# Early weight conversion: ScalarE's pass over the high words in place, VectorE's shift on every second word

## The chip, the cores and the metric

The kernel runs on one core of a Trainium2 chip. The metric is device time in microseconds (us), from the start of the program to its end. Times are compared as medians of several runs.

## The reference

Attention with pooled keys and values, then two feed-forward stages. Weights come as 64-bit floats; the matrix products are carried in two fp32r halves.

```python
def _attn_ref(q, k, v):            # B=8, H=8, S=576, D=64
    k_p = k.reshape(B, H, Sp, pool, D).mean(axis=3)      # pool = 8
    v_p = v.reshape(B, H, Sp, pool, D).mean(axis=3)
    scores = scale * np.matmul(q, k_p.transpose(0, 1, 3, 2))
    ...
    return np.matmul(attn, v_p)
...
def _moe_ref(x, w1, w2, w3, w_out):                      # x: 4608 x 512, d_ff 1024
    return (((x @ w1) * (x @ w2)) @ w3) @ w_out
...
def _moe2_ref(x, w_in, w_out):                           # d_ff 2048
    h = x @ w_in
    return (h * (1.0 / (1.0 + np.exp(-1.702 * h)))) @ w_out
```

## The kernel before, in words

Tokens are worked in nine blocks of 512. The kernel folds `w3 @ w_out` into one matrix first, then runs the blocks through `w1`, `w2` and that matrix (line L583 and on), while the attention of later heads runs beside it in "ticks", and then runs the second feed-forward stage.

**Conversion of the weights.** A weight tile is 128 x 512 numbers of 64 bits, loaded by SyncE (L151) into a slot `t` of shape 128 x 512 x 2 words: the low word and the high word of each number lie side by side. `Conv.step` turns it into fp32 in four operations. ScalarE reads the high words, every second word of the slot, and scales them (L166); ScalarE scales the low words in place (L168); VectorE shifts the result of L166 left by three bits (L169) into a tile `cv`; GpSimd adds the low words (L172). Then the slot is given back. There are four buffers of `cv`. Two steps later the tile is split into a rounded half and a rest (`split`: ScalarE L104, and VectorE or GpSimd L105). For `w3` TensorE transposes it first (L508). In the first stage 40 tiles are converted like this, `w_out`, `w3`, `w1` and `w2`. From the eighth block on `self.ps` holds two PSUM banks, and the result of L166 goes there: 32 more tiles, for the second feed-forward stage.

**Attention.** The work of one pair of heads, in steps that the ticks call: VectorE transposes k and q (L255, L256) and sums keys (L258); TensorE computes scores (L278); VectorE takes the maximum and subtracts (L283, L285); ScalarE takes the exponential (L294); VectorE sums and normalizes (L300 to L303) and transposes (L314, 20 instructions a pair); TensorE multiplies with the values (L380 to L383); ScalarE and VectorE write the result (L390, L391) into a slot that is one quarter of a block of x.

**Blocks.** For each of eight slices f of `w1` and `w2` TensorE does 12 matmuls (L114 to L116) into the bank `wk_70` and 12 into `wk_71`; ScalarE copies the first (L638), VectorE multiplies (L641). The next slice's matmuls into `wk_71` wait for L641.

**Order.** A scheduler builds the program once, from its own model of the timeline: it fixes the order of instructions on each engine, and each engine then works strictly in that order. An instruction that waits holds up everything behind it on its engine. So an edit in one place can move instructions that it doesn't touch.

Of the kernel before, what the change touches and what calls it, by code (L numbers as in the profile page):

```python
# [7 lines left out]
F32 = mybir.dt.float32  # L8
# [14 lines left out]
def pooled_attention_moe_moe2(  # L23
# [71 lines left out]
    def give(*ts):  # L95
        for t in ts:
            if id(t) in held:
                free.append(held.pop(id(t))[1:])
# [28 lines left out]
    class Conv:  # L127
# [27 lines left out]
        def step(self):  # L155

            new = None
            if self.staged:
                t, turn, done = self.staged.pop(0)
                lo_w, hi_w = t[:, :, 0], t[:, :, 1]  # L160
                w = cv_p[0].tile([P, T], F32, name="cv", tag="cv", bufs=4)
                wu = w.bitcast(U32)

                e = self.ps[self.n % len(self.ps)] if self.ps else w
                self.n += 1
                nc.scalar.activation(  # L166
                    e, hi_w.bitcast(F32), AF.Prelu, scale=2.0 ** -112, alpha=-2.0 ** 32)
                nc.scalar.activation(lo_w.bitcast(I32), lo_w, AF.Copy, scale=2.0 ** -29)  # L168
                nc.vector.tensor_scalar(  # L169
                    out=wu, in0=e.bitcast(U32), scalar1=3, scalar2=None,  # L170
                    op0=ALU.logical_shift_left)
                nc.gpsimd.tensor_tensor(  # L172
                    out=w.bitcast(I32), in0=w.bitcast(I32), in1=lo_w.bitcast(I32), op=ALU.add)
                give(t)
                new = [w, turn, done]
            mid, old = self.line
            if mid and mid[1]:
                mid[0] = mid[1](mid[0])
            key = old[2](old[0]) if old else None
            self.line = [new, mid]  # L180
            self.load()
            return key
# [489 lines left out]
    with tc.tile_pool(name="pb", bufs=1, reuse_waits="tile") as pb, \  # L672
# [206 lines left out]
        for k, f in enumerate(FO):  # L879
            bk = bank()  # L880
            w = ready.pop(("h", 0, f))
# [29 lines left out]
        for pr in range(1, NPAIR + 1):  # L911
# [12 lines left out]
            for fp in range(NFP):  # L924
# [4 lines left out]
                for name, i in ORDER:  # L929
# [6 lines left out]
                    if name in PART:  # L936
                        s, h = PART[name]
                        w = ready[s, pr, 2 * fp + i][:, h]
                    else:
                        w = ready[name, pr, fp][:, i]  # L940
# [156 lines left out]
```

## Time and profile before

| | us |
|---|---|
| median of 3 runs (1495.22 to 1498.04) | 1496.11 |
| profiled execution | 1496.16 |
| its span | 1494.0 |
| TensorE busy | 1441.0 |
| VectorE busy | 962.9 |
| ScalarE busy | 693.8 |
| GpSimd busy | 662.1 |

The span runs from the first to the last instruction of the profiled execution; 2.16 us of its time lie around the span. Busy times are shares of that span, and engines overlap.

### The profile page before, as it was taken

The page shows a single profiled execution, that of the slowest core. Times are in us where ns is not written, and L with a number is a line of the kernel's source. Part 1 is how long each engine was busy: PE and PEld are TensorE (multiplying, and loading weights), DVE is VectorE, ACT ScalarE, POOL GpSimd, SP SyncE. Part 2 cuts the span into 40 slices and gives each one's busy share as a digit, 9 for nine tenths or more (in the row PEclk, how much of TensorE's full clock was granted, in tenths as well). Part 3 has the DMA queues.
Part 4 walks back from the last instruction along what each step waited for, and adds up shares of the span by engine and source line. Part 5 has one row for each costly group of instructions (what it writes and reads, how often), then busy time and mean ns, then how long its engine had stood idle before and what let it go on. Part 6 is the DMA issues. An engine that isn't in the chain of part 4 may idle for free.

```text
span 1494.0 us, 19448 instructions
## 1 busy us (share of the span) xinstructions
PE 1441.0 (96%) x6536; PEld 1189.5 (80%) x6536; DVE 962.9 (64%) x1664; ACT 693.8 (46%) x1212; POOL 662.1 (44%) x653
## 2 busy tenths in 40 slices
PE   4988999999999999999999998999999999999998
PEld 3766888888888888888888876778877888788886
DVE  7888998878787877555627255583339433853354
ACT  6974444434343433365635344442455244534442
POOL 7787856555555555366833122500532043302530
PEclk9989999999999999999999999999999999999999
DMA  9991342323232311199879887767676866786665
GB/s 276 242 226 34 65 89 52 77 49 77 48 77 48 76 33 37 61 321 350 307 248 385 285 271 269 272 184 230 198 231 214 230 195 213 230 235 187 200 208 138
DMA packets 292323, 267.64 MB, mean 179 GB/s; under 512 B 199552, under 2 KB 224128, under 8 KB 292224
## 3 DMA queue, kind: packets, MB, share of 16 engines
q1 hardware_dynamic: 291648, 265.35, 59.0%
q10 hardware_dynamic: 576, 1.05, 0.2%
q8 instruction: 52, 0.85, 0.2%
q14 instruction: 47, 0.39, 0.1%
HBM read 209.72 MB, written 56.62 MB: 178 GB/s over the span
## 4 chain that ended last, share of the span: by engine, by line
PE 83%; DVE 6%; DMA 5%; ACT 2%; issue 2%; POOL 2%; SPq 0%; DVEq 0%; POOLq 0%; ACTq 0%
PE bk L709 38%; PE wk L114 8%; PE wk L116 8%; PE wk L115 8%; PE acc L114 5%; PE acc L116 4%; PE acc L115 4%; PE wk L278 2%; DMA xM<-x2d 2%; PE bk L115 1%; PE bk L116 1%; PE bk L114 1%; POOL cv L172 1%; DVE p L314 1%; DMA st<-wud 1%
## 5 line engine op out<-in xcount | busy, mean ns | idle before, releaser
L709 PE MATMUL bk<-mv,st 128*128 128x512 f32 x1104 | 263.6, 394 | 9.6 <-DVE mv L105 4.6
L709 PE MATMUL bk<-xM,st 128*128 128x512 f32 x1140 | 268.4, 390 | 1.9 <-ACT u L962 1.9
L709 PEld LDWEIGHTS bk<-mv,st 128*128 128x128 f32 x1104 | 209.2, 190 | 56.3 <-DVE mv L105 5.9
L709 PEld LDWEIGHTS bk<-xM,st 128*128 128x128 f32 x1140 | 214.4, 188 | 46.9 <-ACT u L962 2.3
L114 PE MATMUL wk<-s,s 128*128 128x512 f32 x576 | 228.1, 398 | 6.5 <-DVE a L641 3.8
L987 POOL TENSOR_TENSOR s<-g,s 128x1024 f32<-128x1024 f32 x16 | 38.8, 2423 | 426.0 <-ACT g L858 426.0
L115 PE MATMUL wk<-s,s 128*128 128x512 f32 x576 | 225.5, 392 | 0.1
L116 PE MATMUL wk<-s,s 128*128 128x512 f32 x576 | 225.3, 392 | 0.1
L314 DVE STREAM_TRANSPOSE p<-s_t 32x160 f32<-32x160 f32 (+1 forms) x560 | 178.5, 319 | 10.5
L105 POOL TENSOR_TENSOR s<-a,s 128x512 fp32r<-128x512 f32 x56 | 73.4, 1310 | 155.0 <-ACT s L104 121.2
L116 PE MATMUL acc<-s,s 128*128 128x512 f32 x352 | 139.4, 396 | 1.8 <-DVE s L105 1.8
L105 DVE TENSOR_TENSOR mv<-g,mv 128x1024 fp32r<-128x1024 f32 x80 | 112.9, 1411 | 43.8 <-ACT mv L104 42.6
L115 PE MATMUL acc<-s,s 128*128 128x512 f32 x352 | 139.5, 396 | 1.2 <-POOL s L105 1.1
L114 PE MATMUL acc<-s,s 128*128 128x512 f32 x352 | 131.9, 400 | 7.6 <-DVE s L105 4.5
L114 PEld LDWEIGHTS wk<-s,s 128*128 128x128 f32 x576 | 108.9, 189 | 30.8 <-DVE a L641 5.0
L116 PEld LDWEIGHTS wk<-s,s 128*128 128x128 f32 x576 | 108.7, 189 | 23.3 <-DVE s L105 0.5
L115 PEld LDWEIGHTS wk<-s,s 128*128 128x128 f32 x576 | 108.6, 189 | 22.2 <-DVE s L391 0.5
L172 POOL TENSOR_TENSOR cv<-cv,s 128x512 int32<-128x512 int32 x72 | 100.8, 1409 | 34.1 <-DVE cv L169 22.4
L104 ACT CAST mv<-g 128x1024 fp32r<-128x1024 f32 x80 | 84.1, 1053 | 64.9 <-PE bk L709 62.3
L114 PEld LDWEIGHTS acc<-s,s 128*128 128x128 f32 x352 | 66.7, 190 | 22.2 <-ACT s L104 5.0
L116 PEld LDWEIGHTS acc<-s,s 128*128 128x128 f32 x352 | 66.8, 190 | 15.6 <-DVE s L105 3.0
L115 PEld LDWEIGHTS acc<-s,s 128*128 128x128 f32 x352 | 66.8, 190 | 14.5 <-POOL s L105 2.3
(188 smaller groups left out, 2469.6 us busy)
## 6 DMA issues: line engine op xcount, KB each, us to landing
st<-wud SPq DMA_DIRECT2D x92, 512.0 KB, 4.2
st<-wind SPq DMA_DIRECT2D x66, 512.0 KB, 4.7
st<-wind SPq DMA_DIRECT2D x84, 256.0 KB, 4.0
s<-in_moe_w_dram SPq DMA_DIRECT2D x32, 512.0 KB, 6.2
wind<-s SPq DMA_DIRECT2D x32, 512.0 KB, 5.2
s<-in_moe_w_out_dram SPq DMA_DIRECT2D x24, 512.0 KB, 6.8
s<-wud SPq DMA_DIRECT2D x20, 512.0 KB, 4.5
kr<-in_k_dram SPq DMA_DIRECT2D x128, 72.0 KB, 2.5
```

What stands on the lines that cost most here:

```text
L104: nc.scalar.copy(dst[:, 0], src)
L105: lo_eng.tensor_tensor(out=dst[:, 1], in0=src, in1=f32(dst[:, 0]), op=ALU.subtract)
L114: nc.tensor.matmul(o, a[:, 0, a_sl], b[:, 0, b_sl], start=first, stop=False)
L115: nc.tensor.matmul(o, a[:, 0, a_sl], b[:, 1, b_sl], start=False, stop=False)
L116: nc.tensor.matmul(o, a[:, 1, a_sl], b[:, 0, b_sl], start=False, stop=last)
L172: nc.gpsimd.tensor_tensor(out=w.bitcast(I32), in0=w.bitcast(I32), in1=lo_w.bitcast(I32), op=ALU.add)
L278: nc.tensor.matmul(sc[half][:, i * KW:(i + 1) * KW], qT[:, sl(tt)], mov, start=True, stop=True)
L314: nc.vector.transpose(out=dst[:, :nt, 32 * c:32 * c + 32], in_=s_t[32 * c:32 * c + 32, :nt, 32 * r:32 * r + 32])
L709: nc.tensor.matmul(o, w[:, x, m], b[:, y], start=first and n == 0, stop=last and n == 2, skip_group_check=True)
L987: nc.gpsimd.tensor_tensor(out=o, in0=p, in1=m, op=ALU.subtract)
```

## The change

The result of L166 is written over the high words that it reads, in the slot, in place of going to the `cv` tile. VectorE's shift L169 then reads every second word of the slot and writes the `cv` tile, which is first used there. Where `self.ps` is set, nothing changes.

```diff
                 w = cv_p[0].tile([P, T], F32, name="cv", tag="cv", bufs=4)
                 wu = w.bitcast(U32)
 
-                e = self.ps[self.n % len(self.ps)] if self.ps else w
+                e = (self.ps[self.n % len(self.ps)] if self.ps else hi_w).bitcast(F32)
                 self.n += 1
                 nc.scalar.activation(
                     e, hi_w.bitcast(F32), AF.Prelu, scale=2.0 ** -112, alpha=-2.0 ** 32)
```

The scheduler builds another order from it. The first place is on TensorE, around the first block's first slice. `s_456`, `s_576`, `s_703` and `s_815` are the four quarters of that block of x; `ph`, `pt` and `vm`, `vt` belong to the attention that yields `s_815`; `s_1148` and `s_1173` are the first slice's weights.

```order
@@ -274,14 +274,6 @@
 L116 MATMUL wk_70<-s_703,s_1148 128x512
 L278 MATMUL wk_73<-kbd,qT 128x144 x2
-L380 MATMUL acc_68<-ph,vm 128x288
-L381 MATMUL acc_68<-ph,vm 128x288
-L380 MATMUL acc_69<-ph,vm 128x288
-L381 MATMUL acc_69<-ph,vm 128x288
 L114 MATMUL wk_71<-s_456,s_1173 128x512
 L115 MATMUL wk_71<-s_456,s_1173 128x512
-L382 MATMUL acc_68<-ph,vm 128x288
-L382 MATMUL acc_69<-ph,vm 128x288
-L383 MATMUL acc_68<-pt,vt 128x288
-L383 MATMUL acc_69<-pt,vt 128x288
 L278 MATMUL wk_72<-kbd,qT 128x144 x3
```

The eight matmuls of that attention stood ahead of `L278 wk_72`, which waits for a transposed q. They now come seven matmuls of 512 columns behind it:

```order
 L116 MATMUL wk_71<-s_703,s_1173 128x512
+L380 MATMUL acc_68<-ph,vm 128x288
+L381 MATMUL acc_68<-ph,vm 128x288
+L380 MATMUL acc_69<-ph,vm 128x288
+L381 MATMUL acc_69<-ph,vm 128x288
+L278 MATMUL wk_73<-kbd,qT 128x144 x2
+L382 MATMUL acc_68<-ph,vm 128x288
+L382 MATMUL acc_69<-ph,vm 128x288
+L383 MATMUL acc_68<-pt,vt 128x288
+L383 MATMUL acc_69<-pt,vt 128x288
 L114 MATMUL wk_70<-s_815,s_1148 128x512
```

So they are the last thing on TensorE before the first matmul that needs their result.

The second place is VectorE's queue at the same point of the program. Before, the two L391 that write `s_815` stand ahead of the maxima of the next scores, and the product L641 of the first slice comes nine rows behind them:

```order
130 L169 TENSOR_SCALAR cv<-cv 128x512
131 L105 TENSOR_TENSOR s_1444<-cv,s_1444 128x512
132 L300 TENSOR_REDUCE nm<-s_t 128x10
133 L283 TENSOR_REDUCE nm<-wk_73 128x4
134 L256 STREAM_TRANSPOSE qT<-qr 128x576
135 L391 TENSOR_TENSOR s_824<-acc_69,s_824 128x64
136 L258 TENSOR_REDUCE ks<-kT 128x72
137 L169 TENSOR_SCALAR cv<-cv 128x512
138 L641 TENSOR_TENSOR a<-wk_71,a 128x512
139 L301 TENSOR_SCALAR nm<-nm 128x10
```

Of the change:

```order
139 L283 TENSOR_REDUCE nm<-wk_73 128x4
140 L256 STREAM_TRANSPOSE qT<-qr 128x576
141 L258 TENSOR_REDUCE ks<-kT 128x72
142 L301 TENSOR_SCALAR nm<-nm 128x10
143 L105 TENSOR_TENSOR s_1581<-cv,s_1581 128x512
144 L255 STREAM_TRANSPOSE kT<-kr 128x576
145 L302 RECIPROCAL nm<-nm 128x10
146 L169 TENSOR_SCALAR cv<-s_1176 128x512
147 L391 TENSOR_TENSOR s_815<-acc_68,s_815 128x288
148 L391 TENSOR_TENSOR s_815<-acc_69,s_815 128x224
149 L303 TENSOR_TENSOR s_t<-s_t,nm 128x5x144
150 L391 TENSOR_TENSOR s_824<-acc_69,s_824 128x64
```

The L391 of `s_815` have moved from ahead of that L283 to eight instructions behind it. The third place follows on directly on VectorE: the first L641 now stands behind the 20 transposes of a pair of heads, of which these are the last.

```order
158 L314 STREAM_TRANSPOSE p_984<-s_t 32x4x32 x2
159 L314 STREAM_TRANSPOSE p_985<-s_t 32x5x32 x2
160 L314 STREAM_TRANSPOSE p_985<-s_t 32x4x32 x2
161 L641 TENSOR_TENSOR a<-wk_71,a 128x512
162 L169 TENSOR_SCALAR cv<-s_1241 128x512
163 L169 TENSOR_SCALAR cv<-s_1251 128x512
```

Before, both the first and the second L641 stood ahead of these transposes.

## Rows read from the trace of the kernel before

**Rows 1.** The page: span, and busy time of each engine.

```profile
span 1494.0 us, 19448 instructions
...
PE 1441.0 (96%) x6536; PEld 1189.5 (80%) x6536; DVE 962.9 (64%) x1664; ACT 693.8 (46%) x1212; POOL 662.1 (44%) x653
```

**Rows 2.** Busy time by stretch, then granted TensorE clock, DMA share, GB/s.

```profile
80.00:100.00 20.00, 17.69 (x78) 14.10 (x79) 17.53 (x24) 15.54 (x34) 18.29 (x22) 0.91 0.99 218
100.00:120.00 20.00, 15.47 (x59) 11.73 (x59) 17.79 (x29) 13.27 (x30) 16.05 (x21) 0.83 0.85 178
...
200.00:300.00 100.00, 100.00 (x481) 84.26 (x482) 86.88 (x214) 42.13 (x96) 58.28 (x81) 1.00 0.30 62
...
800.00:1494.00 694.00, 673.23 (x2937) 553.10 (x2935) 361.06 (x393) 298.35 (x392) 185.62 (x74) 0.99 0.72 227
```

**Rows 3.** Waits of TensorE to 180 us: total us, times, longest.

```profile
PE wk L508 <- POOL cv L172: 11.9, 3, 9.3
...
PE wk L114 <- DVE a L641: 3.8, 2, 1.9
```

**Rows 4.** The conversion's lines, each by itself: ns min/median/max.

```profile
L166 ACT ACTIVATE cv<-s x40: 642/668/693, 4.9 to 138.0; 128x512 f32<-128x512 f32 x40
L168 ACT ACTIVATE s<-s x72: 647/666/697, 5.5 to 728.4; 128x512 int32<-128x512 uint32 x72
L169 DVE TENSOR_SCALAR cv<-cv x40: 359/537/4302, 5.6 to 147.4; 128x512 uint32<-128x512 uint32 x40
L169 DVE TENSOR_SCALAR cv<-wk x32: 675/681/692, 632.6 to 745.7; 128x512 uint32<-128x512 uint32 x32
```

**Rows 5.** Groups of VectorE, 0 to 160 us: busy us, mean ns.

```profile
L169 DVE TENSOR_SCALAR cv<-cv 128x512 uint32<-128x512 uint32 x40 | 36.8, 929 | 10.1 <-ACT cv L166 10.1
```

**Rows 6.** GpSimd in order of time: start, us.

```profile
123.49 1.28 POOL L105 TENSOR_TENSOR s<-a,s 128x512 fp32r<-128x512 f32 x1
```

**Rows 7.** VectorE in order of time.

```profile
105.88 0.76 DVE L256 STREAM_TRANSPOSE qT<-qr 128x576 f32<-128x576 f32 x1
...
109.93 0.74 DVE L391 TENSOR_TENSOR s<-acc,s 128x288 fp32r<-128x288 f32 x2
...
113.70 0.44 DVE L283 TENSOR_REDUCE nm<-wk 128x4 f32<-128x288 f32 x1
...
117.70 1.26 DVE L105 TENSOR_TENSOR s<-cv,s 128x512 fp32r<-128x512 f32 x1
118.88 0.20 DVE L302 RECIPROCAL nm<-nm 128x10 f32<-128x10 f32 x1
120.76 4.30 DVE L169 TENSOR_SCALAR cv<-cv 128x512 uint32<-128x512 uint32 x1 [1.68 <-ACT cv L166]
124.98 1.16 DVE L303 TENSOR_TENSOR s_t<-s_t,nm 128x720 f32<-128x720 f32 x1
...
126.52 0.68 DVE L641 TENSOR_TENSOR a<-wk,a 128x512 f32<-128x512 f32 x1
127.12 6.64 DVE L314 STREAM_TRANSPOSE p<-s_t 32x160 f32<-32x160 f32 x20
```

**Rows 8.** The chain that ended last, followed from 96 to 130 us.

```profile
101.91 3.08 DMA qr<-in_q_dram
```

**Rows 9.** TensorE in order of time; in brackets the wait before.

```profile
106.79 1.78 PE L278 MATMUL wk<-kbd,qT 128*128 128x144 f32 x6 [2.07 <-DVE qT L256]
...
111.85 1.05 PE L114 MATMUL wk<-s,s 128*128 128x512 f32 x2
...
113.37 0.49 PE L115 MATMUL wk<-s,s 128*128 128x512 f32 x1
...
118.85 0.39 PE L114 MATMUL wk<-s,s 128*128 128x512 f32 x1
...
127.26 0.50 PE L114 MATMUL wk<-s,s 128*128 128x512 f32 x1 [1.90 <-DVE a L641]
...
147.53 0.50 PE L114 MATMUL wk<-s,s 128*128 128x512 f32 x1 [1.92 <-DVE a L641]
```

## The prediction

> **What bounds the kernel now.** The page comes first: TensorE is busy for 1441.0 of the 1494.0 us [rows 1], so what matters is where its other 53 us lie. The table by stretch answers that [rows 2]: from 200 to 300 us TensorE works for 100.00 of 100 us, and from 800 to the end for 673.23 of 694. The second figure leaves 21 us idle, in the second feed-forward stage, where the edit changes nothing (`self.ps` is set there). So the time that this change can win or lose lies in the first 200 us, and a lateness that TensorE takes out of them it keeps to the end, unless an idle place in the same stretch takes it back. From 80 to 100 us the DMA engines are busy for 0.99 of the time and from 100 to 120 us for 0.85: until there the loads set the pace. The waits of TensorE up to 180 us come next [rows 3]: 11.9 us before the transposes L508 of `w3`, and 3.8 us, in two waits, before the L114 that want `wk_71` back from L641. TensorE in order of time shows these two at 127.26 (1.90) and 147.53 (1.92), and one of 2.07 before the scores at 106.79 [rows 9]. That last one is for the transposed q of L256 (105.88), whose data lands at 101.91 + 3.08 = 104.99 [rows 7, 8]. An engine that is early before 105 us meets this DMA and gains nothing, and one that is late by up to 2.07 us loses nothing. Hence I follow the order behind 105 us and leave the reordering before it at nothing.
>
> **The change, part by part.** *ScalarE's pass.* L166 now writes every second word in place. L168 has that very shape (it reads and writes every second word) and takes 666 ns in the median, L166 now takes 668 [rows 4]: nothing.
>
> *VectorE's shift.* No row of the trace has VectorE reading every second word, so I bound it. The form in use, from `cv` to `cv`, takes 359 ns at least, 537 in the median, 4302 at most [rows 4], and 929 in the mean of the 40, together 36.8 us within the first 160 us [rows 5]. The spread is a wait inside the instruction. The one of 4.30 us begins at 120.76 and ends at 125.06, just behind a GpSimd subtraction that runs from 123.49 to 124.77 [rows 6, 7]. The form that reads PSUM lies within 675 to 692 ns in all 32 cases [rows 4]: slower by itself, never held. So the lower bound for the 40 new reads is the PSUM form's price without any wait, 40 x (929 - 681) = 9.9 us of VectorE less; the upper one is the slower read with today's waits kept, 40 x (681 - 359) = 12.9 us more. I take the price of today, 537 alone and 929 with the waits, because source and destination are still both in SBUF, as in the row with the wide spread, and only the step differs.
>
> The Trainium skill ("Vector Engine (DVE) Microarchitecture Reference", section 5.1, Performance modes) says that an operation with one source runs at two elements a cycle, over both ports, when source and destination lie in SBUF; the step is not among its conditions. "SBUF — State Buffer", section Who interferes with whom, says that such an operation and a GpSimd operation exclude each other. Here the trace agrees, by the 4.30 us beside the GpSimd row; that a step of two words keeps the mode, no row shows. By these pages the 40 reads cost what they do now, which speaks against a gain of VectorE's.
>
> *The wait for a `cv` buffer* moves from L166 on ScalarE to L169 on VectorE. Behind L169 stand maxima, transposes and L641. With four buffers and tiles freed two steps later I put it at nothing: in the timeline, the waits in front of L169 are for ScalarE (1.68 us at 120.76), not for a buffer [rows 7].
>
> *The order.* This is the part with a price. On TensorE the attention matmuls that yield `s_815` move behind `L278 wk_72`, which waits for the q at 104.99. On VectorE the two L391 that write `s_815` move from ahead of `L283 wk_73` (they ran at 109.93, that L283 at 113.70 [rows 7]) to eight instructions behind it. The first L641 moves behind the 20 transposes. Step by step:
> 1. q lands at 104.99; L256 starts at 105.0 (now 105.88). The L278 come 0.91 behind its start, as now (106.79 - 105.88 [rows 7, 9]): 105.9.
> 2. From there to the L114 of `s_815` TensorE needs 5.06 us (106.79 to 111.85 [rows 9]): 111.0. In their place now stand the first four attention matmuls, 288 columns each. Two L114 of 512 columns take 1.05 us [rows 9]; four of 288 are 1152 columns against 1024, and at a shorter pass I take 1.1: an estimate. Then `L278 wk_73`; today its maximum L283 starts at 113.70, 1.85 behind the L114 at 111.85, or 0.80 behind the 1.05 of the two. So L283 starts at 111.0 + 1.1 + 0.8 = 112.9.
> 3. VectorE then works through L283 0.44, L256 0.76, L258 0.76 (taken as L256, same number of columns), L301 0.20 (taken as L302), L105 1.26, L255 0.76 (as L256), L302 0.20, L169 0.54, and the L391 pair 0.74 [rows 4, 7]: 5.66. Neighbours overlap by about 0.08 (126.52 + 0.68 against 127.12 [rows 7]), nine times 0.7 in all. `s_815` is ready at 112.9 + 5.0 = 117.9. Now the pair ends at 110.67, and TensorE reads `s_815` from 111.85 on and goes on with it at 113.37 [rows 9]. I expect about 4 us of waiting there.
> 4. Behind it L303 1.16, an L391 of 64 columns 0.2 (as L302), and the 20 transposes, 6.64 [rows 7], less the overlaps: L641 starts at 125.6. TensorE follows 0.74 behind it (126.52 to 127.26 [rows 7, 9]): 126.35. That is the first matmul that needs `wk_71` free again, now at 118.85 without a wait [rows 9]. It is 7.5 us late.
> 5. What comes back: the transposes are now done earlier, so the next L641 no longer stand behind them, and the waits at 127.26 and 147.53 go: 1.90 + 1.92 = 3.8 us [rows 9]. Other idle time I see none to take from before 200 us.
>
> Sum: 7.5 - 3.8 = 3.7 us. The profiled execution takes 1494.0 + 2.16 = 1496.16 us, 0.05 above the median of the runs, so 1499.9; I say 1500.0. Without waits inside L105 and L169 it would be 0.8 less (1.26 to 0.68, the length of the L641 of the same size, and 537 to 359 ns [rows 4, 7]); if only one of the two waits goes, 1.9 more; if a shift in the queue ahead of `s_815` is held as long as the 4.30 us one, 3.8 more (4.30 - 0.54). The case's own range is 1499 to 1504.
>
> **The rivals.** A difference under 0.2%, or 3.0 us, can't be told from no change.
> - *No change.* The reordering pulls loads forward, and the q of step 1 lands earlier. For it: ScalarE no longer waits for `cv`. Against it: with 0.99 and 0.85 of the DMA engines busy, only 0.2 and 3.0 us of the 40 us from 80 to 120 can be won [rows 2]. All of it won gives 1500.0 - 3.2 = 1496.8. It decides from 0.9 us on, where the 3.8 falls under 3.0.
> - *Faster.* A read of every second word doesn't run in the form that waits for GpSimd, but as the one from PSUM: 681 ns, never held. All 9.9 us of VectorE on the path give 1500.0 - 9.9 = 1490.1. For it: VectorE is what the chain of steps 3 and 4 runs on, and the 4.30 us at 120.76 lie right before the L641 that TensorE awaits [rows 7]. Against it: both operands stay in SBUF. It comes out faster from 6.9 us on the path (3.9 + 3.0). The sign: L169 of at least 640 ns in the median with none over 700.
> - *Slower by more.* L169 is held often where `s_815` waits behind it, or the slow read keeps its waits as well (12.9 us in all): from 1504.5 up to 1500.0 + 12.9 = 1512.9. For it: the 4.30 us at 120.76 [rows 7]. Against it: the median of 537 ns, most tiles are hardly held [rows 4].
>
> The skill's rule on the two-port form, by which a strided read is still held by GpSimd, has its place in the forecast, and its failure is the second rival.
>
> **How the numbers follow.** Forecast, slower at about 1500.0: 0.50; slower by more: 0.05; no change at about 1496.8: 0.27; faster at about 1490: 0.18. That gives slower 0.55, same 0.27, faster 0.18. Cases of both signs hold much of the chance, so the range reaches from 1492.5, the upper part of the faster case, whose lower part (0.14) stays out, to 1504.5, beyond which lie 0.05.
>
> **What would show it.** Right: a wait of some 4 us before the L114 to L116 that read `s_815`, near 114 to 118 us; another of some 4 us before the first matmul into `wk_71` of the second slice, for an L641 that starts near 125.6 behind the last L314; the waits at 127.26 and 147.53 gone; L169 from the slot spread from about 360 ns to over 1000; from 200 us on every instruction of TensorE later by one constant. Wrong: the first L278 of `wk_72` well before 105 us (first rival); L169 all within 640 to 700 ns (second); waits on `cv` in front of L169, or VectorE over 975 us busy (third). The step I trust least is 5: the order changes further on as well, and idle time that I don't see may take the rest.

## The result: 10 us slower, about half of it in each stage

| | before | changed |
|---|---|---|
| median, us (6 runs each) | 1497.07 (1495.22 to 1501.84) | 1507.11 (1503.48 to 1509.88) |
| ratio of the changed kernel | | 1.0063, interval 1.0042 to 1.0084 |
| profiled execution, us | 1496.16 | 1506.55 |
| span, us | 1494.0 | 1504.8 |

The change is slower by more than its interval, the sign that was forecast, but 2.6 us above the range. The page of the changed kernel, beside [rows 1]:

```profile
span 1504.8 us, 19473 instructions
...
PE 1445.7 (96%) x6536; PEld 1194.1 (79%) x6536; DVE 960.1 (64%) x1664; ACT 694.9 (46%) x1212; POOL 660.4 (44%) x653
```

TensorE does the same 6536 matmuls in 4.7 us more, and stands idle for 59.1 us (1504.8 - 1445.7) where it was 53.0: together the 10.8 us of the span. The table by stretch (columns as in [rows 2]) shows where the first part lies. Before, from 120 us on:

```profile
120.00:140.00 20.00, 18.10 (x80) 14.50 (x79) 17.66 (x32) 8.86 (x17) 18.49 (x18) 1.00 0.11 24
```

and changed, from 100 us on:

```profile
100.00:120.00 20.00, 13.07 (x51) 9.81 (x49) 16.83 (x25) 12.66 (x29) 18.78 (x22) 0.79 0.81 173
120.00:140.00 20.00, 15.48 (x61) 12.09 (x62) 18.87 (x49) 7.57 (x15) 17.03 (x18) 0.87 0.18 35
140.00:160.00 20.00, 20.00 (x98) 16.93 (x97) 14.97 (x34) 8.79 (x22) 18.74 (x30) 1.00 0.28 59
```

From 100 to 120 us TensorE is busy for 13.07 us, not 15.47 [rows 2], and the granted clock is lower: 0.79 there (before 0.83) and 0.87 from 120 to 140 us (before 1.00). To split the loss I take the first matmul of the second feed-forward stage, the first L709 on an `s` slot, as a milestone. The view of that line for the kernel before (min/median/max of the duration in ns, then the first and the last start):

```profile
L709 PE MATMUL bk<-s,s x36: 389/389/389, 769.2 to 831.5; 128*128 128x512 f32 x36
```

and for the changed kernel:

```profile
L709 PE MATMUL bk<-s,s x36: 389/389/389, 774.4 to 836.7; 128*128 128x512 f32 x36
```

So 5.2 us are lost before it, and from it to the end of the span it takes 730.4 us (1504.8 - 774.4) in place of 724.8: 5.6 us more, in a stage whose code is untouched. How much of this is idle time shows in the two stretches, ahead of the milestone and behind it. Before:

```profile
0.00:769.20 769.20, 736.99 (x3465) 610.86 (x3466) 587.91 (x1255) 376.73 (x791) 467.93 (x573) 0.99 0.47 129
769.20:1494.00 724.80, 704.03 (x3073) 578.62 (x3071) 374.96 (x410) 317.09 (x422) 194.22 (x80) 0.99 0.73 233
```

and changed:

```profile
0.00:774.40 774.40, 740.02 (x3465) 614.25 (x3466) 580.50 (x1255) 377.46 (x791) 466.18 (x573) 0.98 0.47 128
774.40:1504.80 730.40, 705.70 (x3073) 579.88 (x3071) 379.65 (x410) 317.42 (x422) 194.19 (x80) 0.99 0.72 231
```

Of the 5.2 us ahead of the milestone only 2.2 are more idle time; the other 3.0 are the same 3465 matmuls taking longer. All of it arises before 200 us: from there to the milestone TensorE is idle for less than 0.1 us in either kernel, with a granted clock of 1.00. Up to 200 us the mean granted clock is 0.93, before 0.96. Behind the milestone 3.9 of the 5.6 us are idle time.

**The first stage.** TensorE of the changed kernel in order of time, at the places of [rows 9]:

```profile
106.51 0.97 PE L278 MATMUL wk<-kbd,qT 128*128 128x144 f32 x6 [0.62 <-ACT s L104]
...
115.27 0.53 PE L383 MATMUL acc<-pt,vt 96*128 96x288 f32 x2 [0.51 <-POOL vt L342]
118.45 1.22 PE L114 MATMUL wk<-s,s 128*128 128x512 f32 x2 [2.64 <-ACT s L390]
121.41 0.79 PE L115 MATMUL wk<-s,s 128*128 128x512 f32 x1 [1.73 <-DVE s L391]
...
123.90 0.63 PE L115 MATMUL wk<-s,s 128*128 128x512 f32 x1
...
130.35 0.50 PE L114 MATMUL wk<-s,s 128*128 128x512 f32 x1 [3.12 <-DVE a L641]
```

and VectorE, beside [rows 7]:

```profile
105.60 0.77 DVE L256 STREAM_TRANSPOSE qT<-qr 128x576 f32<-128x576 f32 x1
...
114.50 0.45 DVE L283 TENSOR_REDUCE nm<-wk 128x4 f32<-128x288 f32 x1
...
117.89 1.73 DVE L105 TENSOR_TENSOR s<-cv,s 128x512 fp32r<-128x512 f32 x1 [1.27 <-ACT s L104]
...
120.61 0.74 DVE L391 TENSOR_TENSOR s<-acc,s 128x288 fp32r<-128x288 f32 x2
121.27 1.60 DVE L303 TENSOR_TENSOR s_t<-s_t,nm 128x720 f32<-128x720 f32 x1
...
122.93 6.64 DVE L314 STREAM_TRANSPOSE p<-s_t 32x160 f32<-32x160 f32 x20
129.60 0.69 DVE L641 TENSOR_TENSOR a<-wk,a 128x512 f32<-128x512 f32 x1
```

The reader sees the forecast chain: TensorE waits 2.64 and 1.73 us for `s_815` (L390, L391), then 3.12 us for the L641 behind the 20 transposes. Its first matmul into the second slice's `wk_71` starts at 130.35, not 118.85 [rows 9]. Behind it the waits of 127.26 and 147.53 are gone.

`s_815` is late because its matmuls now come later on TensorE, and ScalarE adds to it. In the kernel before:

```profile
101.20 0.29 ACT L338 CAST vm<-vf 128x128 fp32r<-128x128 f32 x1
101.39 0.24 ACT L340 CAST vt<-vtf 32x64 fp32r<-32x64 f32 x1
```

and in the changed one:

```profile
106.36 0.29 ACT L338 CAST vm<-vf 128x128 fp32r<-128x128 f32 x1
110.90 0.70 ACT L166 ACTIVATE s<-s 128x512 f32<-128x512 f32 x1 [4.25 <-DMA s<-in_moe_w_dram]
...
114.54 0.23 ACT L340 CAST vt<-vtf 32x64 fp32r<-32x64 f32 x1
```

The scheduler sets conversions ahead of the attention's copies `vm` and `vt`, presumably because L166 no longer waits for a `cv` buffer. One of them then waits 4.25 us for its weights' DMA, and `vt`, queued behind it, comes 13 us later than before. In this execution TensorE's L383 waits only 0.51 us for the rest of `vt` that GpSimd makes from it (L342, above). In three others with the same first-stage order, the experiments below with L826 moved, it waits 4.4 us, and L641 costs 4.0; one of them:

```profile
116.83 0.85 PE L383 MATMUL acc<-pt,vt 96*128 96x288 f32 x2 [4.39 <-POOL vt L342]
```

**The second stage.** VectorE's sums L826, 256 columns each, in the kernel before (pairs; free, a pair takes 0.76 us):

```profile
888.87 0.76 DVE L826 TENSOR_TENSOR ws<-wq 128x256 f32<-128x256 f32 x2
...
913.29 5.00 DVE L826 TENSOR_TENSOR ws<-wq 128x256 f32<-128x256 f32 x2
```

and in the changed kernel, with the L105 behind the first pair:

```profile
892.03 5.02 DVE L826 TENSOR_TENSOR ws<-wq 128x256 f32<-128x256 f32 x2
...
897.76 1.22 DVE L105 TENSOR_TENSOR mv<-s,mv 128x1024 fp32r<-128x1024 f32 x1
...
919.97 4.97 DVE L826 TENSOR_TENSOR ws<-wq 128x256 f32<-128x256 f32 x2
```

GpSimd of the changed kernel in that time:

```profile
886.56 2.40 POOL L987 TENSOR_TENSOR s<-g,s 128x1024 f32<-128x1024 f32 x1 [39.23 <-ACT g L858]
889.03 2.42 POOL L987 TENSOR_TENSOR g<-g,s 128x1024 f32<-128x1024 f32 x1
891.40 2.85 POOL L987 TENSOR_TENSOR g<-g,g 128x1024 f32<-128x1024 f32 x1
894.20 2.57 POOL L1004 TENSOR_TENSOR g<-g,g 128x1024 f32<-128x1024 f32 x1
```

and what TensorE then waits for:

```profile
899.04 2.96 PE L709 MATMUL bk<-mv,s 128*128 128x512 f32 x8 [3.01 <-DVE mv L105]
...
928.11 1.22 PE L709 MATMUL bk<-mv,st 128*128 128x512 f32 x2 [5.86 <-ACT mv L104]
```

Two L826 that begin during GpSimd's four subtractions (886.56 to 896.77) take 5.02 us in place of 0.76. The L105 behind them is late, and TensorE stands still. The second wait comes the same way: behind the held pair at 919.97 stands VectorE's L954, ScalarE's L858 waits 7.97 us for that, and the L104 that TensorE awaits stands behind this L858. In the kernel before the first pair (888.87) began 0.6 us behind the end of such a run, and only the later one met a run. The last instruction of the run that the first pair missed, and TensorE's wait behind the later pair:

```profile
885.90 2.39 POOL L1004 TENSOR_TENSOR g<-g,g 128x1024 f32<-128x1024 f32 x1
...
920.28 4.63 PE L709 MATMUL bk<-mv,st 128*128 128x512 f32 x10 [3.89 <-DVE mv L105]
```

The order says why. On ScalarE, before:

```
L858 ACTIVATE g_8195<-bk_8206 128x512
L858 ACTIVATE g_8193<-g_8193 128x1024
L104 CAST mv<-g_8195 128x1024
L831 CAST wt<-ws 128x2x256
L950 COPY m<-bk_8385 128x512
```

In the changed kernel the L858 of `g_8193`, for which GpSimd's run waits, stands behind that L950, which waits for TensorE:

```profile
884.73 0.59 ACT L950 COPY m<-bk 128x512 f32<-128x512 f32 x1 [1.88 <-PE bk L709]
885.42 1.06 ACT L858 ACTIVATE g<-g 128x1024 f32<-128x1024 f32 x1
```

The run starts at 886.56 in place of 877.39, 9.2 us later, while TensorE is only 5.2 us later there, and so it lands on the L826.

### The profile page after: what moved, and what is told of

It is laid out like the page before. It is cut to its first block, busy times and chain, and to the rows that moved or that the text cites. A ratio compares the mean times of both kernels' runs of the same rounds, so it can differ in the third digit from the quotient of the medians.

```text
span 1504.8 us, 19473 instructions
## 1 busy us (share of the span) xinstructions
PE 1445.7 (96%) x6536; PEld 1194.1 (79%) x6536; DVE 960.1 (64%) x1664; ACT 694.9 (46%) x1212; POOL 660.4 (44%) x653
## 4 chain that ended last, share of the span: by engine, by line
PE 80%; DMA 7%; DVE 5%; POOL 2%; ACT 2%; issue 2%; SPq 1%; POOLq 0%; DVEq 0%; ACTq 0%
PE bk L709 37%; PE wk L114 8%; PE wk L116 8%; PE wk L115 8%; PE acc L114 4%; PE acc L116 4%; PE acc L115 4%; PE wk L278 2%; DMA xM<-x2d 2%; POOL cv L172 1%; DMA s<-in_moe_w_dram 1%; DMA wud<-wt 1%; PE bk L114 1%; PE bk L115 1%; PE bk L116 1%
## 5 line engine op out<-in xcount | busy, mean ns | idle before, releaser
L709 PE MATMUL bk<-mv,st 128*128 128x512 f32 x1104 | 262.8, 393 | 12.7 <-ACT mv L104 9.9
L709 PE MATMUL bk<-xM,st 128*128 128x512 f32 x1140 | 269.6, 390 | 1.4 <-ACT u L962 1.4
L709 PEld LDWEIGHTS bk<-mv,st 128*128 128x128 f32 x1104 | 209.0, 190 | 59.2 <-ACT mv L104 11.2
L709 PEld LDWEIGHTS bk<-xM,st 128*128 128x128 f32 x1140 | 214.7, 188 | 46.5 <-ACT u L962 1.8
L105 POOL TENSOR_TENSOR s<-a,s 128x512 fp32r<-128x512 f32 x56 | 73.0, 1303 | 168.8 <-ACT s L104 133.4
L116 PE MATMUL acc<-s,s 128*128 128x512 f32 x352 | 140.3, 398 | 1.9 <-DVE s L105 1.9
L115 PE MATMUL acc<-s,s 128*128 128x512 f32 x352 | 140.4, 399 | 1.1 <-POOL s L105 1.0
L114 PE MATMUL acc<-s,s 128*128 128x512 f32 x352 | 134.4, 405 | 5.2 <-ACT s L104 2.5
L105 DVE TENSOR_TENSOR mv<-g,mv 128x1024 fp32r<-128x1024 f32 x80 | 113.1, 1414 | 39.6 <-ACT mv L104 38.4
L104 ACT CAST mv<-g 128x1024 fp32r<-128x1024 f32 x80 | 84.3, 1055 | 61.7 <-PE bk L709 58.7
```

Source lines behind the costliest of these rows:

```text
L104: nc.scalar.copy(dst[:, 0], src)
L105: lo_eng.tensor_tensor(out=dst[:, 1], in0=src, in1=f32(dst[:, 0]), op=ALU.subtract)
L114: nc.tensor.matmul(o, a[:, 0, a_sl], b[:, 0, b_sl], start=first, stop=False)
L115: nc.tensor.matmul(o, a[:, 0, a_sl], b[:, 1, b_sl], start=False, stop=False)
L116: nc.tensor.matmul(o, a[:, 1, a_sl], b[:, 0, b_sl], start=False, stop=last)
L709: nc.tensor.matmul(o, w[:, x, m], b[:, y], start=first and n == 0, stop=last and n == 2, skip_group_check=True)
```

## The experiments

The milestone is the first matmul of the second stage in the one profiled execution of each; "rest" is the span less that. A profiled execution can lie up to 4.9 us from its kernel's median, so these two columns tell of that execution alone. Each ratio is to the kernel before, measured beside it.

| run | median, us | ratio (interval) | first L709 | rest |
|---|---|---|---|---|
| before | 1496.3 to 1497.2 | | 769.2 | 724.8 |
| changed | 1507.11 | 1.0063 (1.0042 to 1.0084) | 774.4 | 730.4 |
| strided read alone | 1497.06 | 1.0008 (0.9993 to 1.0024) | 773.3 | 719.7 |
| first 24 tiles in place | 1500.12 | 1.0026 (1.0013 to 1.0039) | 776.2 | 724.3 |
| last 16 tiles in place | 1511.88 | 1.0098 (1.0074 to 1.0121) | 786.0 | 726.4 |
| changed, L826 on GpSimd | 1498.50 | 1.0006 (0.9989 to 1.0022) | 778.4 | 718.6 |
| before, L826 on GpSimd | 1496.03 | 0.9995 (0.9977 to 1.0012) | 771.3 | 719.9 |
| changed, one pair of L826 moved | 1501.75 | 1.0035 (1.0021 to 1.0048) | 779.3 | 722.2 |
| changed, two pairs moved | 1502.52 | 1.0036 (1.0022 to 1.0050) | 777.3 | 724.6 |
| changed, moved L826, attention first | 1503.63 | 1.0043 (1.0023 to 1.0062) | 775.9 | 720.8 |
| the same, priority for the values only | 1504.82 | 1.0059 (1.0039 to 1.0080) | 782.8 | 719.9 |
| before, moved L826, attention first | 1498.28 | 1.0007 (0.9990 to 1.0024) | 778.3 | 722.7 |
| changed, moved L826, L641 ahead | 1505.17 | 1.0048 (1.0034 to 1.0062) | 781.1 | 721.3 |
| before, moved L826, L641 behind | 1509.88 | 1.0077 (1.0063 to 1.0092) | 785.0 | 724.4 |

**The instruction by itself.**

```diff
-                    out=wu, in0=e.bitcast(U32), scalar1=3, scalar2=None,
-                    op0=ALU.logical_shift_left)
+                    out=wu, in0=e.bitcast(U32) if self.ps else hi_w, scalar1=3, scalar2=None,
+                    op0=ALU.logical_shift_left if self.ps else ALU.logical_shift_right)
```

> The kernel before with one edit: VectorE's shift of the 40 early tiles reads every second word of the slot (the high words as they were loaded, shifted right, so the weights are wrong); ScalarE still writes the cv tile, whose result the shift overwrites. The order of every engine is that of the kernel before. Theory (the order costs, the instructions don't): within 2 us of the kernel before, the first L709 within 1.5 us of 769.2, L169 from about 360 ns, held now and then. Rival (the strided read itself costs, by a slower form or by more waiting for GpSimd): 3 us slower or more, and L169 with a minimum above 500 ns or a mean above 929.

No difference that can be measured; the interval leaves at most 0.24%, 3.6 us. Every engine's order is that of the kernel before, so this is the price of the strided read alone. L169 in this kernel (ns min/median/max):

```profile
L169 DVE TENSOR_SCALAR cv<-s x40: 358/428/4531, 5.9 to 151.5; 128x512 uint32<-128x512 uint32 x40
```

and in the changed kernel:

```profile
L169 DVE TENSOR_SCALAR cv<-s x40: 358/436/2104, 5.6 to 132.1; 128x512 uint32<-128x512 uint32 x40
```

At least 358 ns, as with the contiguous source (359 [rows 4]), and still held beside GpSimd. L166 in place takes 678 ns in the median (min 653), against 668: 0.4 us in all 40, the only price of the write in place that the rows show. The instructions cost next to nothing, so the order has to be the cause. The first L709 came at 773.3, outside my 1.5 us: one and the same order gave 769.2, 771.3 and 773.3 in three profiled executions, so a single milestone is good to some 4 us.

**Half of the tiles.**

```diff
-                e = (self.ps[self.n % len(self.ps)] if self.ps else hi_w).bitcast(F32)
+                e = (self.ps[self.n % len(self.ps)] if self.ps else hi_w if self.n >= 24 else w).bitcast(F32)
```

> In place only from the 25th of the 40 early tiles on (w1 and w2); the first 24 go as before. In VectorE's order the first L641 still stands behind the 20 transposes. Theory (the order around the first block costs 5 us): the first L709 at 773 to 776, as in the changed kernel (774.4), against 769.2 before. Rival (the first tiles, w_out and w3, carry the loss): the first L709 within 1.5 us of 769.2.

With `< 24` in the other kernel:

> In place only for the first 24 of the 40 early tiles. In VectorE's order the two L391 of s_815 and the first L641 stand ahead of the 20 transposes, as before. Theory (the order around the first block costs 5 us): the first L709 within 2 us of 769.2. Rival (the first tiles carry the loss): the first L709 at 773 to 776.

Each makes an order of its own. The last 16 tiles alone cost no less than all 40 (786.0; 1.0098, the intervals overlap), so the loss isn't a sum over tiles. The first 24 reach the milestone at 776.2, although there the first L641 does stand ahead of the transposes (TensorE waits 2.66 and 1.24 us for L390 and L391 all the same): my expectation of 769.2 failed, and with it the view that this one place is the whole loss.

**The sums of the second stage on GpSimd.**

```diff
-                    nc.vector.tensor_tensor(out=v[o], in0=x, in1=y, op=op)
+                    nc.gpsimd.tensor_tensor(out=v[o], in0=x, in1=y, op=op)
```

> The changed kernel with the four sums L826 of the second feed-forward stage on GpSimd in place of VectorE; up to the second stage the order is that of the changed kernel. Theory (the second half of the loss is two L826 on VectorE held by GpSimd's subtractions near 892 and 920 us): the first L709 at 774.4 as in the changed kernel, and from there to the end about 721 us (before 724.8, changed 730.4), so some 9 us less than the changed kernel, 1496 to 1499. Rival (the second stage loses by its DMA or the clock): from the first L709 to the end still 728 to 732 us.

> The kernel before with the four sums L826 of the second stage on GpSimd; up to the second stage its order is that of the kernel before. Theory (half of the loss is in each stage): only one pair of L826 is held there (3.9 us), so it gains 3 to 5 us, 1491.5 to 1493.5, and lies about 5 us below the changed kernel with the same edit (1498.5), which is the loss of the first stage. Rival (the second stage has no part in the loss): it gains the 8.6 us that the changed kernel gained, 1487.7.

The same edit takes 8.6 us from the changed kernel (1507.11 to 1498.50) and nothing that can be measured from the kernel before. So the changed kernel loses at these sums, and the kernel before hardly does. I had expected 3 to 5 us there too, but the pair at 913.29 is not always held for 5.00 us. In the run with the strided read alone, whose order is that of the kernel before, it was held for 2.82:

```profile
918.78 2.82 DVE L826 TENSOR_TENSOR ws<-wq 128x256 f32<-128x256 f32 x2
```

and TensorE's waits for the L105 `mv` came to 0.9 us in all, in place of 4.6. With the sums on GpSimd they came to 5.7 us: other L105 were held there, so what the move freed came back.

To see whether the move helps in another way, only the held pairs were moved:

```diff
+                    (nc.gpsimd if f == 4 else nc.vector).tensor_tensor(out=v[o], in0=x, in1=y, op=op)
```

> The changed kernel with the sums L826 of one of the eight weights of the second stage on GpSimd, the one whose pair was held 5.02 us at 892.03; all orders are those of the changed kernel up to that pair. Theory (each held pair makes TensorE wait): the wait of 3.0 us near 899 goes, the second pair may be held as before; 1502 to 1505 against 1507.1. Rival (the sums on GpSimd helped in another way than by the held pairs): 1506 to 1508, since seven of eight stay on VectorE.

> As the run before it, with the second held pair (4.97 us at 919.97) on GpSimd as well. Theory: the waits of 3.0 and 5.9 us of TensorE near 899 and 928 both go, and the time comes to that of the kernel with all eight on GpSimd, 1497 to 1500. Rival: 1505 to 1508.

One pair of the eight gives back 5.4 us (1507.11 to 1501.75; 4.2 by the two ratios, whose intervals overlap). From 885 to 940 us TensorE of that kernel has only these waits:

```profile
924.33 2.57 PE L709 MATMUL bk<-mv,st 128*128 128x512 f32 x10 [0.24 <-DVE mv L105]
...
928.53 9.81 PE L709 MATMUL bk<-xM,st 128*128 128x512 f32 x42 [0.27 <-DVE g L969]
```

The second wait went along with the first, since the second pair now comes at 927.11, behind GpSimd's run, and takes 0.76. But the collision has only moved on. The eighth pair now falls into GpSimd's next run (934.81 to 945.00), and TensorE waits right behind it:

```profile
940.26 5.03 DVE L826 TENSOR_TENSOR ws<-wq 128x256 f32<-128x256 f32 x2
950.24 2.93 PE L709 MATMUL bk<-xM,st 128*128 128x512 f32 x6 [6.15 <-ACT u L962]
```

TensorE's waits in the second stage fall from 18.3 to 12.9 us in all. The second kernel moved a pair that was no longer held and left the eighth, which was held for 5.04 us again, with a wait of 5.22 behind it: hence 1502.52 and not the expected 1497 to 1500. With all eight moved VectorE has no pair left that could be held, and the time is lower than with one (1498.50 against 1501.75). This is the cleanest test of the second stage: the orders are the changed kernel's own up to the first held pair, and in each of these executions a wait of TensorE follows a pair that is held for 5 us.

**What carries the loss of the first stage?** Here the sums are on GpSimd, so that the second stage stays out. First a higher priority for the attention's work in the first four pairs:

```diff
-                    g4(n)
-                    g_va(n)
+                    with tc.high_priority(): g4(n); g_va(n)
                 elif s == 5:
-                    g_vb(n)
+                    with tc.high_priority(): g_vb(n)
```

> The changed kernel with the sums on GpSimd, and with a higher priority for the scheduler on the attention's copies and splits of the first four pairs (L338 to L342, L351 to L372, and the sums of values). In its order the matmuls that yield s_815 stand ahead of L278 wk_72 again, and the first L641 ahead of the 20 transposes. Theory (the conversion, no longer held by cv, gets ahead of the attention's copies, and that is the first stage's loss): as the kernel before with the same sums, 1491 to 1495. Rival (the loss comes from the read in place): as the changed kernel with these sums, 1497 to 1500.

> As the run before it, but without the priority for L351 to L372. The attention's copies L338 to L341 come early, and s_815 with them, but the first and second L641 stand behind the 20 transposes, as in the changed kernel. If L641 behind the transposes is what costs, 1497 to 1500; if the late s_815 is what costs, 1491 to 1495.

> The kernel before with the sums on GpSimd and the priority of the second run: does the priority gain by itself? Theory: the order around s_815 and L641 is about that of the kernel before, so within 2 us of the kernel before with the sums alone (1491.5 to 1493.5). Rival: the priority gains by itself, 1490 or less.

Neither brought the time of the kernel before back: 1503.63 and 1504.82, both above every range that was expected. In the first the first L641 stands ahead of the transposes, but the second doesn't, and TensorE waits 4.5 us for it. In the second TensorE still waits for L390 and L391 (1.60 and 3.73 us) and for L641 (3.72), so it separated nothing. On the kernel before the priority makes no measurable difference. Then the first L641 alone was moved, ahead of the transposes in the changed kernel:

```diff
+            for p in (p0, p1) if n == NPE else (): nc.vector.tensor_copy(p[:, 0, ::32], xs['a'][:p.shape[0], :4])
             for r in range(5):
...
-            if i >= 4 and tick_n[0] < 20:
+            if i >= 4 and tick_n[0] < 19:
...
-        while tick_n[0] < 20:
+        while tick_n[0] < 19:
```

(The line that keeps `a` in `xs` is left out here. One tick of the attention moves from ahead of the blocks to beside them.)

> The changed kernel with the sums on GpSimd, and the 20 transposes of the fifth pair held back (two copies of four columns) until the first L641 is done: in VectorE's order the first L641 now stands ahead of the transposes, the second still behind them; the matmuls of s_815 stay late. Theory of the prediction (the L641 behind the transposes carries the first stage's loss): the wait of 4.0 us before the first matmul of the second slice goes, 1494 to 1496.5, 2 to 4 us under the changed kernel with these sums (1498.5). Rival (the wait moves to the next L641, or the late s_815 carries the loss): 1498 to 1501.

and behind them in the kernel before:

```diff
+                    if (blk, f) == (0, 0): nc.vector.tensor_copy(a[:32, :4], g_s[NPE][1][:, 0, ::32])
                     nc.vector.tensor_tensor(out=a, in0=pb_, in1=a, op=ALU.mult)
```

> The mirror: the kernel before with the sums on GpSimd, and the first L641 held back until the 20 transposes are done (by a copy of four columns into its operand, so a few numbers of the result are wrong); s_815 stays early. Theory of the prediction: a wait of 4 us or more before the first matmul of the second slice, less what the next two L641 give back, 1498 to 1501 against 1496.0 without. Rival (the late s_815 carries the loss): 1495 to 1497.5.

In the first the rival's way came true, though not its time. The wait at the second slice is gone, but the next L641 now stands behind the transposes, and TensorE waits there (L642 is L641, one line down):

```profile
145.87 0.50 PE L114 MATMUL wk<-s,s 128*128 128x512 f32 x1 [3.06 <-DVE a L642]
```

The kernel got slower (1505.17, against 1498.50 without this edit). In the mirror the time went up by 13.9 us (1496.03 to 1509.88), more than expected. More than L641 was late there: TensorE's longest wait now stands before a matmul with the values:

```profile
135.12 0.88 PE L380 MATMUL wk<-ph,vm 128*128 128x288 f32 x2 [10.03 <-ACT pt L371]
```

So it shows that an L641 behind the transposes is dear, but not how dear it is alone.

## Why the prediction was half right

- **What bounds the kernel.** Right that TensorE sets the time, but of the 10.8 us only 6.1 are idle time. The other 4.7 are longer matmuls, 3.0 of them ahead of the milestone, where the granted clock was lower; the sum has no term for that. Wrong in "where the edit changes nothing (`self.ps` is set there). So the time that this change can win or lose lies in the first 200 us": this is the step that failed. The code of the second stage is unchanged, but its order isn't, and there TensorE's waits rest on whether a pair of L826 meets GpSimd's run, which the first pair missed by 0.6 us before. That stage took 5.6 us more, and the runs with the moved L826 show why: 5.4 us for one pair, 8.6 for all. I had read the order only up to the first block.
- **The instructions.** Right: the strided read costs nothing that can be measured (1.0008, interval 0.9993 to 1.0024), the write in place 10 ns each, and the read keeps the fast form that is held beside GpSimd. The rival "faster" fell with it: the median of L169 is 436 ns, not 681. Its 40 shifts took 25.3 us in place of 36.8 all the same, as they were held less often in the new order. That is 11.5 us less, beyond the 9.9 of the lower bound, and the kernel is slower all the same. The wait for a `cv` buffer cost nothing by itself: within the first 160 us L169 waited for L166 (6.6 us), never for a buffer.
- **Steps 1 to 4** name the right places, and each came later than forecast. L256 at 105.60 (forecast 105.0); L283 of `wk_73` at 114.50 (112.9); the L391 pair done at 121.35 (117.9), 1.27 us of it a wait for ScalarE's L104 that I hadn't seen, and 0.47 in an L105 longer than today's (1.73 against 1.26); L641 at 129.60 (125.6); TensorE at 130.35 (126.35). So 11.5 us late, not 7.5. The same 424 matmuls lie ahead of that place in either kernel: 6.5 of the 11.5 us are more idle time, and 5.0 are these matmuls taking longer (96.0 us busy against 91.1, with a mean granted clock of 0.90 against 0.93). The steps took TensorE's matmuls at the lengths of the kernel before.
- **Step 5.** The waits at 127.26 and 147.53 went, 3.8 us, as forecast. 11.5 - 3.8 leaves 7.7, of which the milestone shows 5.2. Of the other 2.5 us, 0.5 are small waits of the kernel before that went too, most of them between 160 and 200 us. The other 2.0 came back in busy time: from that place to the milestone TensorE is busy for 644.0 us in place of 645.9, with the same matmuls left; I can't name the rows. From 200 us to the milestone everything is later by one constant, as forecast; behind the milestone it isn't.
- **The sum for the first stage.** Forecast 3.7, measured 5.2, and that the two lie near each other is in part luck: the chain was 4.0 us later than forecast, 2.5 us more came off, and 3.0 of the 5.2 are longer matmuls. Four profiled executions with the changed kernel's first-stage order give 774.4, 777.3, 778.4 and 779.3, mean 777.4; three with that of the kernel before 771.3: 6.1 us, of which 2.9 are longer busy time of TensorE and 3.2 idle time. By time, the kernel with one pair moved, whose second stage was no longer than before in the profiled executions (722.2 against 724.8), is 0.35% slower, 5.2 us. With all eight moved in both kernels the difference is only 2.5 us (1498.50 against 1496.03), and their intervals overlap. Some 5 us is what most of the runs say, with 2.5 and 6.1 as the ends.
- **What stays open.** Which of the moved instructions carries the first stage's loss. The rows show `s_815` and L641 in the chain, but undoing either, or both, made orders with new waits of the same size. What the lower clock in the first stage hangs on was not tried either. The seven other orders that were tried reached the second stage at 775.9 us or later in the one execution profiled of each, that of the kernel before at 769.2 to 773.3. By their times six of the seven are slower too; the kernel before with the priority is not (1.0007). That ScalarE's freedom from `cv` is what sets conversions ahead of the attention is read from the order and from ScalarE's rows; no run shows it by itself.

## What to carry to other kernels

Where a scheduler sets the order, compare the order on every engine to the end of the program, not only where the edit lies, and look in every later stage for pairs of engines that hold each other up. A wait that is taken from an engine may have been a gate that kept other work in front (here that is read from the order, not shown): ask what will run ahead of what. Count busy time as well as idle time, since a late matmul can also be a longer one. Where a wait goes, look further on for the place where it comes back. Six of seven other orders came out slower here, so the first one was probably a lucky one, and an edit has to be judged at equal order, as the strided read was.

## What the runs showed of the hardware

- VectorE's shift of 512 words reads every second word as fast as contiguous ones (358 against 359 ns at the shortest), and is held by GpSimd in both forms (up to 4531 and 4302 ns).
- A two-input instruction on VectorE is held as well. The pair of L826 takes 0.76 us free and 5.02 beside GpSimd's subtractions, about one GpSimd instruction (2.4 to 2.9 us) for each of the two. "SBUF — State Buffer" of the Trainium skill, section Who interferes with whom, says that a VectorE instruction with two inputs in SBUF contends with a GpSimd instruction that reads SBUF; the trace agrees, by these rows.
- Around its waits TensorE lost twice. From 110 to 125 us most 512-column matmuls of the changed kernel last 0.63 us, not 0.39, with the granted clock at 0.79 and 0.87 of full speed (so partly at the lower of its two levels, 1.2 and 2.4 GHz), after waits of 0.6 to 2.6 us; that is part of the 4.7 us by which its busy time grew. Not every wait does this: after that of 3.12 us at 130.35 they last 0.39 to 0.50.
- Executions of one and the same order differed by 4 us at the milestone and by 5 us behind it (724.8 against 719.7 for the order of the kernel before), with the length of single holds between VectorE and GpSimd among the causes: the hold of 5.00 or 2.82 us goes with waits of 4.6 or 0.9 us on TensorE.
